# Attention and soft mixture of experts on one core: z loads at the batch turn, another order of v's low parts, x's shifts in a row

## The chip, the core and the metric

The kernel runs on one core of a Trainium2 chip. Its engines each work through a program of their own, in order: TensorE (PE in the profile, with its weight loads as PEld), VectorE (DVE), ScalarE (ACT), GpSimd (POOL) and SyncE (SP), which here issues the DMA transfers. They wait for one another by semaphores. The metric is the time of one execution in microseconds (us), the median over several runs.

## What is computed

Two stages, one behind the other. The first is an attention without softmax for 8 batches of 2496 tokens with 256 features: the scores are the products of z (64 features) with itself, cut at zero and squared, then multiplied with v and gated by u. The second is a soft mixture of experts over all 19968 rows of the first: 32 slots (8 experts with 4 each), with one softmax over the tokens to fill the slots, and another over the slots to give each token its output.

```python
def _attn_ref(u, v, z):
    scores = (1.0 / S) * np.matmul(z, z.transpose(0, 2, 1))
    attn = np.maximum(scores, 0.0) ** 2
    return u * np.matmul(attn, v)
...
def _moe_ref(x, phi, w1, w2):
    logits = x @ phi
    d = np.exp(logits - logits.max(0, keepdims=True))
    d /= d.sum(0, keepdims=True) + 1e-09
    slot_input = (d.T @ x).reshape(E, S_per_e, D)
    ...
    c = np.exp(logits - logits.max(1, keepdims=True))
    c /= c.sum(1, keepdims=True) + 1e-09
    return c @ slot_out
```

The numbers are single precision at the border. Inside, z, v and the squared scores are each kept as two 16-bit parts, a high one and a low one (what the high one has lost).

## The kernel before, in words

**Half steps.** A batch is worked in 5 chunks of up to 512 tokens as queries, and each chunk meets 5 blocks of 512 keys, each in two halves: 50 half steps per batch, numbered through the whole kernel, so that batch b begins at half step 50 b. A half step multiplies v (high and low part) with the squared scores (`ph` high, `pl` low) and adds the result up in PSUM (`acc`). PE's rows are `acc<-ph,v` and `acc<-pl,v`.

**Scores ahead.** While half step h is summed up, half step h+3 is prepared (`prepare`). PE makes the scores (`sc<-z,z`) in the middle of the sums of h. ACT cuts them at zero (`r<-sc`), squares them (`r<-r`) and casts the high part (`ph<-r`; in some half steps DVE casts). DVE subtracts the low part (`pl<-r,ph`). The tile `sc` exists once: the scores of the next half step are not written before ACT has read those of the last.

**Fetched half steps.** The scores are symmetric. DVE turns many `r` tiles around (`y<-r`), they are stored in DRAM (`turned<-y`) and later fetched as the mirrored half step (`r<-turned`), which then needs no scores. Quarter steps are lent and borrowed in the same way (`yd`, `lent`, `rd`).

**The second stage between the half steps.** When 1024 rows of x are there (`xg`, the gated sum, written by DVE at the end of a chunk), a group of the second stage starts. It has a list `todo`; one item is taken out per half step, as long as the half step is not among the first two of its chunk. Most items only put a function on one of two lists: `middle` is run in `prepare` right behind the next cut at zero, before its square, so on ACT; `behind` is run at the end of `prepare`, so behind the subtraction and the turning on DVE. The items are: `logits` (PE: x times phi, row `lg<-xg`, with the sums of the group before, `lg<-xt`, ahead of or behind them), `ex` (the first exp), four `blocks` and `e` (DVE turns x and the exponentials, `y<-xg`), four `shifts` (each four DMAs of 72 KB, `xt<-y`, by which x reaches the rows that the next sums need), `c0` the *combine* (three DVE operations on the tile `L`: a transposition, a maximum, a subtraction), `c1` the second exp (`L<-L` on ACT), `c2` sum and division, `c3` a last transposition. There are 18 groups with this list, each some 20 half steps behind the last.

**Loads of the next batch.** While batch b−1 runs, z and v of batch b are loaded (`zr<-in_zz`, `vr<-in_v`, 256 KB each, 12 places). A table gives the start (issue, two half steps ahead of it), and the half steps of what follows: for z the largest value (`sq<-zr`, DVE), then the split into parts; for v the squares, the high part on ACT (`v<-vr,v_by`) and the low part on DVE (`v<-vr,v_by,v`). In the code `base` is 50 (b−1).

**What sets the order.** Every engine's program is the order in which the code writes it, kept as it stands by a helper in line 78, so nearly all rows of the profile name that line. In a half step the code first does the transfers (`transfers(h)`, all on SP's queue, in order), then takes one item of a group's list, then adds the table's work that lands on this half step to `behind`, then writes the sums with the preparation of h+3 between:

```python
transfers(h)
if work and (x.at > 1 or last <= 20):
    work.pop(0)()
weights(last)
behind.extend(landing.pop(h, ()))
...
turn = sums_halves(h, acc, 0, None)
prepare(ahead.pop(0))
sums_halves(h, acc, 1, turn)
```

The lines that the change touches are 794 (the list of a group) and 903 to 906 (high and low parts of v, start of z).

Of the kernel before, what the change touches and what calls it, by code (L numbers as in the profile page):

```python
# [81 lines left out]
def attn_soft_moe_kernel(ctx, tc, uT, v, zz, zh, phi, ww, outT):  # L82
# [83 lines left out]
    def add_bounds(b, ps, js):  # L166
        pe.matmul(
            ps[:, 0, js], nc.const_aps.tensor(1.0, [P, P], F32), tops[b % 2][:, js], start=True, stop=True
        )

    def factors(b, ps, js):


        n2, by = (t[b % 2][:, js] for t in (norm2, z_by))
        dve.tensor_scalar(bits(n2), bits(ps[:, 0, js]), EVEN, None, op0=ALU.bitwise_and)
        dve.tensor_scalar(
            bits(by), bits(n2), EVEN, 1, op0=ALU.bitwise_xor, op1=ALU.logical_shift_right
        )
        dve.tensor_scalar_mul(by, by, 2.0**77)
# [25 lines left out]
    def largest(b):  # L205


        root, w = v_by[b % 2], few[b % 2]
        n2 = norm2[b % 2].unsqueeze(2).to_broadcast([P, NP, 2])
        dve.tensor_scalar(  # L210
            bits(root), bits(energy[b % 2]), 1, ROOT, op0=ALU.logical_shift_right, op1=ALU.bitwise_and
        )
        r2 = root.rearrange("p (j i) -> p j i", i=2)
        dve.tensor_tensor_reduce(
            r2, r2, n2, 1.0, 2.0**-120, op0=ALU.mult, op1=ALU.max, accum_out=w[:, 0:1]
        )

    def scale_v(b, ps):


        w = few[b % 2]
        ps = ps[:, :, 2 * PAD :]
        for h, rows in enumerate(HALF):
            pe.matmul(
                ps[:, h], w[rows, 0:1].to_broadcast([64, P]), ident[rows, rows],
                start=True, stop=True,
            )
        dve.tensor_reduce(w[:, 1:2], ps, axis=AX.XY, op=ALU.max)
        dve.tensor_scalar(
            bits(w[:, 2:3]), bits(w[:, 1:2]), EXPONENT, EXPONENT, op0=ALU.bitwise_and, op1=ALU.bitwise_xor  # L230
        )
        n2 = norm2[b % 2].unsqueeze(2).to_broadcast([P, NP, 2])
        dve.tensor_scalar(
            v_by[b % 2].rearrange("p (j i) -> p j i", i=2), n2, w[:, 2:3], 2.0**-51, op0=ALU.mult, op1=ALU.mult
        )
        dve.tensor_scalar(
            out_by[b % 2], norm2[b % 2], w[:, 1:2], 2.0**40 / S**2, op0=ALU.mult, op1=ALU.mult
        )
# [363 lines left out]
    def finish_chunk(b, ch, acc):  # L602
        j, _, n, t0 = ch
        ut = ut_.pop(t0)
        s = 0
        while s < n:
            q, o = divmod(t0 + s, 1024)
            w = min(n - s, 1024 - o)
            if q not in xg_:
                xg_[q] = wk.tile([P, 2, 1024], F32, tag="xg", name=f"xg_{q}")  # L610
            for c in (slice(0, 1), slice(1, 2)) if t0 + n == N else (slice(0, 2),):
                dve.scalar_tensor_tensor(
                    xg_[q][:, c, o : o + w], acc[:, c, s : s + w], out_by[b % 2][:, j : j + 1],
                    ut[:, c, s : s + w], op0=ALU.mult, op1=ALU.mult,
                )
            if o + w == 1024:
                work.extend(groups(q))
            s += w
# [17 lines left out]
    def shift(src, a):  # L636


        for b in range(4):
            sp.dma_start(xt[32 * b : 32 * b + 32, a], src[32 * a : 32 * a + 32, b])  # L640

    def groups(q):
# [48 lines left out]
        def turn_block(j, c):  # L691
            dve.transpose(
                y()[:, :, j * D : (j + 1) * D].rearrange("p b (t c f) -> p c t b f", t=4, c=2)[:, c],
                x[:, c, 512 * j : 512 * (j + 1)].rearrange("p (t b k) -> p t b k", t=4, b=4),
            )
# [50 lines left out]
        def turn_x_whole(i):  # L746
            j, t0 = i // 2, i % 2 * 2
            ps = ms_ps.tile([P, 2, 512], F32, tag="ms", name=f"xt_{q}_{i}")
            for k in range(2):
                turn_x(ps[:, k], x, 4 * j + t0 + k)  # L750
            for k in range(2):
                copy_x(act.copy, ps[:, k, 0:D], xt[:, t0 + k, j * D : (j + 1) * D])
# [34 lines left out]
        blocks = [lambda j=j, c=c: behind.append(lambda: turn_block(j, c)) for j in range(2) for c in range(2)]  # L787
        shifts = [lambda a=a: shift(y(), a) for a in range(4)]
        e, c0, c2, c3 = (lambda f=f: behind.append(f) for f in (turn_e, combine, combine_sum, combine_turn))
        ex, c1 = (lambda f=f: middle.append(f) for f in (exps, combine_exp))  # L790
        rest = lambda: None
        if q < NQG - 2:

            todo = [logits, ex, *blocks, e, *shifts[0:2], c0, *shifts[2:4], c1, c2]
            todo.append(lambda: (c3(), late.append(slot_sums)))
        else:


            todo = [rest, rest, logits, ex, lambda: behind.append(adding.pop(0)), lambda: behind.append(add_counts)]
            todo += [c0, c1, c2, c3, turn_e_whole, *[lambda i=i: turn_x_whole(i) for i in range(4)]]  # L800
            todo.append(lambda: late.append(last_slot_sums))
# [95 lines left out]
    splits, later = {}, {}  # L897
    for b in range(1, B):
        base, order = (b - 1) * 2 * NP * NQ, BLOCKS[b == B - 1]
        z_at = [28, 29, 30, 31, 39]  # L900
        v_from = [6, 7, 8, 9, 24, 25, 26, 31, 32, 33]
        v_sq = [17, 18, 19, 20, 28, 29, 30, 32, 33, 33]
        v_high = [43, 41, 41, 42, 42, 43, 44, 44, 45, 45]
        v_low = [47, 42, 43, 44, 45, 46, 48, 49, 50, 51]
        for i, (j, at) in enumerate(zip(order, z_at)):
            splits.setdefault(base + 9 + 2 * i, []).append((load_z, b, j, [base + 12 + 2 * i, base + at]))
        for i, (start, *steps) in enumerate(zip(v_from, v_sq, v_high, v_low)):
            splits.setdefault(base + start, []).append((load_v, b, i, [base + at for at in steps]))
        later[base + 23] = lambda b=b: add_bounds(b, next_acc(), slice(0, NP))
        later[base + 24] = lambda b=b: factors(b, accs[-1], slice(0, NP))  # L910
        later[base + 36] = lambda b=b: largest(b)
        later[base + 39] = lambda b=b: scale_v(b, ms_ps.tile([P, 2, 512], F32, tag="ms", name=f"mx_{b}"))
# [3 lines left out]
    def next_acc():  # L916

        accs.append(acc_ps.tile([P, 2, QC], F32, tag="acc", name=f"acc_{len(accs)}"))
        return accs[-1]
# [217 lines left out]
    for t in range(4):  # L1137
        pe.matmul(
            ep_[t * NS : (t + 1) * NS, 0:D], ET[:, t * NS : (t + 1) * NS], xt_last[t],
            start=True, stop=True,  # L1140
# [222 lines left out]
```

## Time and profile before

| | |
|---|---|
| median of 3 runs | 1285.04 us (1284.22 to 1287.97) |
| the profiled execution, its own time | 1285.79 us |
| its span | 1284.0 us |
| instructions on PE, DVE, ACT | 10987, 1582, 1211 |
| DMA | 299.41 MB, mean 233 GB/s |
| largest row: `acc<-ph,v` on PE, 5036 matmuls | 927.4 us |
| `acc<-pl,v` on PE, 2518 matmuls | 599.0 us |
| `pl<-r,ph` on DVE, 412 subtractions | 468.0 us |

The time of a row is its busy time. Matmuls overlap in the pipeline, so the rows of one engine may add up to more than the span. In a row of the timeline the columns are the start, the duration, the engine and the line, the operation with what it writes and reads, the shape and the count; a bracket at the end tells how long the engine had been idle before, and what it waited for. Rows of equal operations that follow each other are drawn together (x4). A wait "A <- B" in the list of waits says that the engine of A was idle until B was done.

### The profile page before, as it was taken

The page shows a single profiled execution, that of the slowest core. Times are in us where ns is not written, and L with a number is a line of the kernel's source. Part 1 is how long each engine was busy: PE and PEld are TensorE (multiplying, and loading weights), DVE is VectorE, ACT ScalarE, POOL GpSimd, SP SyncE. Part 2 cuts the span into 40 slices and gives each one's busy share as a digit, 9 for nine tenths or more (in the row PEclk, how much of TensorE's full clock was granted, in tenths as well). Part 3 has the DMA queues.
Part 4 walks back from the last instruction along what each step waited for, and adds up shares of the span by engine and source line. Part 5 has one row for each costly group of instructions (what it writes and reads, how often), then busy time and mean ns, then how long its engine had stood idle before and what let it go on. Part 6 is the DMA issues. An engine that isn't in the chain of part 4 may idle for free.

```text
span 1284.0 us, 27704 instructions
## 1 busy us (share of the span) xinstructions
PE 1250.8 (97%) x10987; PEld 597.8 (47%) x10987; DVE 1095.7 (85%) x1582; ACT 934.1 (73%) x1211; POOL 5.2 (0%) x23
## 2 busy tenths in 40 slices
PE   9999999999999999999999999999999999999984
PEld 3444444444444444444444444444444444445752
DVE  7888998889988899789998799898998899886663
ACT  7877786778866888677867778577876778564543
POOL 1000000000000000000000000000000000000000
PEclk9999999999999999999999999999999999999985
DMA  5768658774888758785787747877477758889869
GB/s 180 256 185 267 199 150 267 245 244 137 239 276 247 246 136 240 249 242 172 197 275 219 268 138 221 267 238 248 134 250 254 259 158 225 251 277 320 313 257 382
DMA packets 136546, 299.41 MB, mean 233 GB/s; under 512 B 17888, under 2 KB 38880, under 8 KB 124384
## 3 DMA queue, kind: packets, MB, share of 16 engines
q1 hardware_dynamic: 136416, 297.64, 73.1%
q8 instruction: 86, 1.41, 0.5%
q14 instruction: 44, 0.36, 0.1%
HBM read 162.56 MB, written 113.77 MB: 215 GB/s over the span
## 4 chain that ended last, share of the span: by engine, by line
PE 73%; DMA 9%; DVE 7%; ACT 5%; SPq 3%; issue 2%; ACTq 0%; DVEq 0%; POOLq 0%
PE acc L78 59%; PE sc L78 9%; SPq L78 3%; DMA r<-turned 3%; DVE pl L78 2%; PE lg L78 2%; DMA vr<-in_v 2%; PE pf L78 2%; DVE y L78 2%; ACT r L78 2%; DMA xt<-y 1%; DMA w_own<-in_w 1%; ACT ot L78 1%; ACT ph L78 1%; DMA turned<-y 1%
## 5 line engine op out<-in xcount | busy, mean ns | idle before, releaser
L78 PE MATMUL acc<-ph,v 64*128 64x512 f16 (+5 forms) x5036 | 927.4, 368 | 1.5 <-DVE v L78 1.2
L78 PEld LDWEIGHTS <-v 64*128 64x128 f16 (+1 forms) x7554 | 461.8, 95 | 531.6 <-issue 37.2
L78 PE MATMUL acc<-pl,v 64*128 64x512 f16 (+5 forms) x2518 | 599.0, 368 | 1.8 <-DVE pl L78 1.5
L78 DVE TENSOR_TENSOR pl<-r,ph 128x1024 f16<-128x1024 f32 (+1 forms) x412 | 468.0, 1141 | 110.6 <-ACT ph L78 88.2
L78 ACT CAST ph<-r 128x1024 f16<-128x1024 f32 (+1 forms) x286 | 289.5, 1016 | 147.5 <-DMA r<-turned 112.1
L78 ACT ACTIVATE r<-sc 128x1024 f32<-128x1024 f32 (+1 forms) x230 | 217.7, 947 | 107.0 <-PE sc L78 100.6
L78 ACT ACTIVATE r<-r 128x1024 f32<-128x1024 f32 (+1 forms) x242 | 238.5, 986 | 6.8
L78 DVE STREAM_TRANSPOSE y<-r 128x1024 f32<-128x1024 f32 x160 | 198.0, 1237 | 0.0
L78 PE MATMUL sc<-z,z 64*128 64x512 f16 x912 | 123.4, 376 | 1.5 <-ACT r L78 1.4
L78 PEld LDWEIGHTS <-z 64*128 64x128 f16 x1380 | 68.0, 94 | 75.8 <-issue 2.3
L78 DVE CAST ph<-r 128x1024 f16<-128x1024 f32 (+1 forms) x123 | 73.0, 594 | 14.5 <-ACT r L78 14.3
L78 ACT ACTIVATE v<-vr,v_by 128x512 f16<-128x512 f32 (+1 forms) x81 | 53.8, 707 | 10.2 <-DVE v_by L78 10.2
L78 DVE SCALAR_TENSOR_TENSOR xg<-acc,out_by,ut 128x1024 f32<-128x1024 f32 (+7 forms) x57 | 51.7, 929 | 8.4 <-PE acc L78 8.4
L78 DVE SCALAR_TENSOR_TENSOR v<-vr,v_by,v 128x512 f16<-128x512 f32 (+1 forms) x81 | 58.1, 718 | 0.0
L78 ACT ACTIVATE vq<-vr 128x512 bf16<-128x512 f32 x75 | 46.8, 623 | 15.5 <-DMA vr<-in_v 15.1
L78 PE MATMUL sc<-z 64*128 64x512 f16 (+1 forms) x468 | 50.6, 321 | 0.0
L78 DVE STREAM_TRANSPOSE y<-xg 128x512 f32<-128x512 f32 x72 | 49.4, 686 | 0.0
L78 DVE COPY ot<-pf 128x1024 f32<-128x1024 f32 (+1 forms) x20 | 24.0, 1198 | 20.5 <-PE pf L78 20.5
L78 ACT COPY ot<-pf 128x1024 f32<-128x1024 f32 (+1 forms) x20 | 19.8, 991 | 24.2 <-PE pf L78 24.2
L78 DVE TENSOR_TENSOR pl<-rd,ph 128x512 f16<-128x512 f32 x36 | 23.7, 660 | 6.4 <-ACT ph L78 6.4
L78 DVE SCALAR_TENSOR_TENSOR z<-zr,z_by,z 128x512 f16<-128x512 f32 x35 | 25.8, 737 | 0.0
L78 DVE STREAM_TRANSPOSE yd<-r 128x512 f32<-128x512 f32 x36 | 25.3, 704 | 0.0
(188 smaller groups left out, 541.8 us busy)
## 6 DMA issues: line engine op xcount, KB each, us to landing
turned<-y SPq DMA_DIRECT2D x320, 256.0 KB, 5.2
r<-turned SPq DMA_DIRECT2D x76, 1024.0 KB, 7.2
xt<-y SPq DMA_DIRECT2D x288, 72.0 KB, 4.2
vr<-in_v SPq DMA_DIRECT2D x80, 256.0 KB, 4.6
outT<-ot SPq DMA_DIRECT2D x18, 1024.0 KB, 6.7
ut<-in_uT SPq DMA_DIRECT2D x31, 512.0 KB, 6.6
lent<-yd SPq DMA_DIRECT2D x144, 64.0 KB, 2.6
rd<-lent SPq DMA_DIRECT2D x36, 256.0 KB, 5.0
```

The costliest lines, as they stand in the source:

```text
L78: return lambda *a, **k: self.tc.keep_in_program_order(f(*a, **k))
```

## The change

```diff
-            todo = [logits, ex, *blocks, e, *shifts[0:2], c0, *shifts[2:4], c1, c2]
+            todo = [logits, ex, *blocks, e, *shifts, c0, c1, c2]
...
-        v_high = [43, 41, 41, 42, 42, 43, 44, 44, 45, 45]
-        v_low = [47, 42, 43, 44, 45, 46, 48, 49, 50, 51]
+        v_high = [41, 43, 41, 42, 42, 43, 44, 44, 45, 45]
+        v_low = [42, 49, 43, 44, 45, 46, 46, 48, 52, 47]
         for i, (j, at) in enumerate(zip(order, z_at)):
-            splits.setdefault(base + 9 + 2 * i, []).append((load_z, b, j, [base + 12 + 2 * i, base + at]))
+            start = base + i - 1 if base else 9 + 2 * i
+            splits.setdefault(start, []).append((load_z, b, j, [base + 12 + 2 * i, base + at]))
```

In a group's list, shifts 2 and 3 come one half step earlier, and the combine comes two half steps later, directly ahead of the second exp, which keeps its place. Of v, part 0 is split earlier (low part at step 42 instead of 47 of the batch before), part 1 later (49 instead of 42), and parts 6 to 9 at 46, 48, 52 and 47 instead of 48, 49, 50 and 51. Of z, for batches 2 to 7, the five loads are issued at half steps base−3 to base+1 instead of base+7 to base+15; what is done with them stays where it was.

On DVE, in batch 2 around half step 106, group 3 (its `L` has the number 3819; `pl` and `y` with 43.. and 44.. are the half steps 107, 108 and 109). Before:

```order
L78 STREAM_TRANSPOSE L_3819<-L_3819 128x256
L78 TENSOR_REDUCE rm_3729<-L_3819 128x8
L78 TENSOR_TENSOR L_3819<-L_3819,rm_3729 128x256
L78 TENSOR_TENSOR pl_4316<-r_4305,ph_4315 128x1024
L78 STREAM_TRANSPOSE y_4319<-r_4305 128x2x16x32
L78 TENSOR_TENSOR pl_4368<-r_4357,ph_4367 128x1024
L78 STREAM_TRANSPOSE y_4319<-r_4357 128x2x16x32
L78 TENSOR_TENSOR pl_4411<-rd_4176,ph_4410 128x8x64
```

The same place now:

```order
L78 TENSOR_TENSOR pl_4327<-r_4316,ph_4326 128x1024
L78 STREAM_TRANSPOSE y_4330<-r_4316 128x2x16x32
L78 TENSOR_TENSOR pl_4375<-r_4364,ph_4374 128x1024
L78 STREAM_TRANSPOSE y_4330<-r_4364 128x2x16x32
L78 STREAM_TRANSPOSE L_3819<-L_3819 128x256
L78 TENSOR_REDUCE rm_3729<-L_3819 128x8
L78 TENSOR_TENSOR L_3819<-L_3819,rm_3729 128x256
L78 TENSOR_TENSOR pl_4421<-rd_4200,ph_4420 128x8x64
```

The three operations on `L` have moved behind the subtractions and transpositions of two half steps. ACT's rows around the second exp stand as before; here they are in the kernel now, where `r_4364` is half step 108 and `r_4409` half step 109:

```order
L78 CAST ph_4374<-r_4364 128x1024
L78 ACTIVATE r_4409<-sc_4410 128x2x256
L78 ACTIVATE L_3819<-L_3819 128x256
L78 ACTIVATE r_4409<-r_4409 128x2x256
L78 CAST ph_4420<-rd_4200 128x8x64
L78 ACTIVATE r_4456<-sc_4457 128x1024
```

The exp reads what the combine's subtraction writes, as it did, and the rest of ACT's work for half steps 109 and 110 stands behind it.

On DVE ahead of the turn at half step 150, from the low part of v5 to the gated rows `xg`. Before:

```order
L78 SCALAR_TENSOR_TENSOR v_5_4281<-vr_5_5068,v_by_90,v_5_4281 128x2x256
L78 CAST ph_5914<-r_5904 128x1024
...
L78 SCALAR_TENSOR_TENSOR v_0_4276<-vr_0_4286,v_by_90,v_0_4276 128x2x256
...
L78 SCALAR_TENSOR_TENSOR v_6_4282<-vr_6_5117,v_by_90,v_6_4282 128x2x256
...
L78 SCALAR_TENSOR_TENSOR v_7_4283<-vr_7_5332,v_by_90,v_7_4283 128x2x256
L78 SCALAR_TENSOR_TENSOR xg_5349<-acc_5716,out_by_91,ut_5753 128x2x128
```

And now:

```order
L78 SCALAR_TENSOR_TENSOR v_5_3965<-vr_5_5068,v_by_90,v_5_3965 128x2x256
L78 SCALAR_TENSOR_TENSOR v_6_3966<-vr_6_5118,v_by_90,v_6_3966 128x2x256
L78 CAST ph_5927<-r_5917 128x1024
...
L78 SCALAR_TENSOR_TENSOR v_9_3969<-vr_9_5381,v_by_90,v_9_3969 128x2x256
...
L78 SCALAR_TENSOR_TENSOR v_7_3967<-vr_7_5332,v_by_90,v_7_3967 128x2x256
...
L78 SCALAR_TENSOR_TENSOR v_1_3961<-vr_1_4344,v_by_90,v_1_3961 128x2x256
L78 SCALAR_TENSOR_TENSOR xg_5349<-acc_5716,out_by_91,ut_5753 128x2x128
```

Between the cast of half step 150 and `xg` stand three low parts in both, and two instead of one right ahead of that cast; v0 is not among them any more.

On SP's queue in the first steps of batch 2, where z of batch 3 is loaded. Before, z stands between the stores and fetches there:

```order
L78 DMA vr_2_4384<-in_v 128x512
L78 DMA zr_0_4428<-in_zz 128x512
L78 DMA vr_3_4430<-in_v 128x512
L78 DMA turned_0_4_4432<-y_4319 32x4x512 x4
L78 DMA lent_1_4476<-yd_4462 32x4x128 x4
L78 DMA zr_1_4523<-in_zz 128x512
L78 DMA rd_4571<-lent_1_4476 128x512
L78 DMA r_4614<-turned_0_1_4128 128x2048
L78 DMA zr_2_4616<-in_zz 128x512
```

Now the loads stand ahead of the batch's first stores:

```order
L78 DMA zr_0_3970<-in_zz 128x512
L78 DMA zr_1_4015<-in_zz 128x512
L78 DMA lent_0_4017<-yd_3999 32x4x128 x4
L78 DMA zr_2_4065<-in_zz 128x512
L78 DMA xt<-y_3874 32x576 x4
L78 DMA zr_3_4108<-in_zz 128x512
L78 DMA zr_4_4151<-in_zz 128x512
L78 DMA turned_0_1_4153<-y_4049 32x4x512 x4
```

The five loads have left the stretch with the fetches `r` and come behind the turn of the batch.

## The prediction

> **What bounds the kernel now.** I read the head of the page first, then the list of waits, then the timeline at the places that the change touches.
>
> ```profile
> span 1284.0 us, 27704 instructions
> ...
> PE 1250.8 (97%) x10987; PEld 597.8 (47%) x10987; DVE 1095.7 (85%) x1582; ACT 934.1 (73%) x1211; POOL 5.2 (0%) x23
> ...
> PEclk9999999999999999999999999999999999999985
> ...
> PE 73%; DMA 9%; DVE 7%; ACT 5%; SPq 3%; issue 2%; ACTq 0%; DVEq 0%; POOLq 0%
> ```
>
> TensorE (PE) is busy for 97% of the span at a granted clock of 0.9 or more in all slices but the last two, and the change takes no matmul away. So the kernel can only get faster where PE stands still, and gets slower wherever PE is made to stand. VectorE (DVE) at 85% and ScalarE (ACT) at 73% have room on average; what counts is whether they are late at one given matmul. The waits (total us, times, longest):
>
> ```profile
> ACT ph L78 <- DMA r<-turned: 112.1, 34, 8.5
> ACT r L78 <- PE sc L78: 102.1, 92, 3.8
> ...
> ACT L L78 <- DVE L L78: 7.6, 3, 3.0
> ...
> PE lg L78 <- DMA xt<-y: 2.0, 2, 1.3
> ...
> PE sc L78 <- ACT r L78: 1.4, 2, 1.1
> ...
> PE acc L78 <- DVE v L78: 1.2, 3, 0.7
> ...
> PE lg L78 <- DVE xg L78: 0.7, 1, 0.7
> ```
>
> The last four rows are PE's: 5.3 us in eight stalls (counted between starts, about 7 us, since the matmuls around a stall also stretch). They are at the four kinds of place that this change works on: the last shift of x (`xt<-y`), the scores' single tile (`sc<-z`), the low part of v0 at the batch turn, and the gated rows `xg`. That is all that the change can win in the middle of the kernel.
>
> The first two rows are the cover: ACT has often nothing to do until PE has made the next scores, or until a fetched `r` has landed. The third is the sign of danger: in 3 of its groups ACT's second exp (`L<-L`) already waits for the three combine operations of DVE.
>
> **The change part by part.** *Part 1, four shifts in a row, combine behind them.* The combine (a transpose, a reduce and a subtract on `L`) moves two half steps later; the exp that reads its result stays where it is. The instructions are the same, 19 times each:
>
> ```profile
> L78 ACT ACTIVATE L<-L x19: 398/407/417, 131.7 to 1192.7; 128x256 f32<-128x256 f32 x19
> ```
>
> Of these, 18 belong to groups with the changed list. Groups are some 20 half steps long and batches 50, so the exp falls on steps 6, 26, 46, 16 and 36 of a batch in turn; the eighteenth, behind the others, waits for nothing. I take step 6 first, group 3, where the exp stands at half step 106. First DVE, then ACT, then PE:
>
> ```profile
> 332.61 0.40 DVE L78 STREAM_TRANSPOSE L<-L 128x256 f32<-128x256 f32 x1
> 333.05 0.42 DVE L78 TENSOR_REDUCE rm<-L 128x8 f32<-128x256 f32 x1
> 333.50 0.42 DVE L78 TENSOR_TENSOR L<-L,rm 128x256 f32<-128x256 f32 x1
> 333.85 1.22 DVE L78 TENSOR_TENSOR pl<-r,ph 128x1024 f16<-128x1024 f32 x1
> 334.98 1.24 DVE L78 STREAM_TRANSPOSE y<-r 128x1024 f32<-128x1024 f32 x1
> ...
> 337.24 1.23 DVE L78 STREAM_TRANSPOSE y<-r 128x1024 f32<-128x1024 f32 x1
> ```
>
> ```profile
> 333.98 1.04 ACT L78 CAST ph<-r 128x1024 f16<-128x1024 f32 x1
> 334.93 0.59 ACT L78 ACTIVATE r<-sc 128x512 f32<-128x512 f32 x1
> 335.42 0.41 ACT L78 ACTIVATE L<-L 128x256 f32<-128x256 f32 x1
> 335.73 0.62 ACT L78 ACTIVATE r<-r 128x512 f32<-128x512 f32 x1
> 336.25 0.60 ACT L78 CAST ph<-rd 128x512 f16<-128x512 f32 x1
> 337.78 1.02 ACT L78 ACTIVATE r<-sc 128x1024 f32<-128x1024 f32 x1 [0.92 <-PE sc L78]
> ```
>
> ```profile
> 339.73 0.81 PE L78 MATMUL sc<-z,z 64*128 64x512 f16 x6
> ```
>
> Now the combine is done at 333.9 and the exp finds it ready at 335.42. Afterwards DVE starts `pl` of half step 107 at 332.61, in the combine's place. The `pl` of 108 must wait for ACT's cast, which ends at 335.02, so it runs to 336.2, its transpose to 337.4, and only then comes the combine, 1.24 us from 332.61 to 333.85 by the rows, now 337.4 to 338.65. The exp starts at 338.70, **3.3 us later**. Behind it on ACT, in program order, stand the square, the cast of the fetched half and the relu of the next scores. From the exp's start to that relu the rows need 0.31 + 0.52 + 0.52 = 1.35 us, so the relu begins at 340.05 instead of 337.78 and ends at 341.07. ACT's own wait of 0.92 us is used up and 2.3 us are left over. The score tile has one copy: PE's next scores, due at 339.73, must wait until this relu has read it. The old relu ended at 338.80, so 0.93 us of lateness were free; 1.4 us become a stall of PE. That such a wait stops PE at once shows in a place of before:
>
> ```profile
> 719.68 1.00 ACT L78 ACTIVATE r<-sc 128x1024 f32<-128x1024 f32 x1
> ...
> 720.74 0.61 PE L78 MATMUL sc<-z,z 64*128 64x512 f16 x4 [1.08 <-ACT r L78]
> ```
>
> The relu ended at 720.68 and the scores came 0.06 us later. Step 6 comes four times (groups 1, 3, 8, 13), with the same rhythm of rows: 4 × 1.4 = **+5.6 us**. Bounds: 4 if DVE gains 0.4 us each time, 6.4 if the matmuls after a stall stretch by 0.2 us.
>
> At steps 26 and 36 the DVE transposition behind which the combine now lands begins at, for example,
>
> ```profile
> 576.94 1.24 DVE L78 STREAM_TRANSPOSE y<-r 128x1024 f32<-128x1024 f32 x1
> ```
>
> ```profile
> 694.99 1.24 DVE L78 STREAM_TRANSPOSE y<-r 128x1024 f32<-128x1024 f32 x1
> ```
>
> and the exp, at 576.16 and 694.21 before, comes near 579.5 and 697.5. But the half steps that follow there use fetched `r` and need no scores, so the score tile is no limit; late are only the casts `ph` and the subtractions `pl` of the half step with the fetched half. Following the rows by the same rule, PE waits about 0.9 us at each of the three steps 26, and has its later stalls there shrunk by nearly as much, as PE itself then comes later: +1.2 together. Steps 36 (groups 0, 2, 7, 12): 0.3, 0.3, 1.1, 0.7, together +2.4. At step 16 the exp waits already, and ACT idles for its fetches there:
>
> ```profile
> 513.07 0.42 DVE L78 TENSOR_TENSOR L<-L,rm 128x256 f32<-128x256 f32 x1
> ...
> 513.53 0.42 ACT L78 ACTIVATE L<-L 128x256 f32<-128x256 f32 x1 [2.33 <-DVE L L78]
> ```
>
> I put it at +0.5 for all three. Bounds of these ten places: 0.5 to 8 us.
>
> *Part 2, low parts of v.* Ten subtractions per batch as before; only the order changes. Before, the turns at half steps 150 and 350 looked so (DVE, then PE):
>
> ```profile
> 460.19 0.75 DVE L78 SCALAR_TENSOR_TENSOR v<-vr,v_by,v 128x512 f16<-128x512 f32 x1
> ...
> 467.03 1.27 DVE L78 SCALAR_TENSOR_TENSOR xg<-acc,out_by,ut 128x256 f32<-128x256 f32 x2
> ```
>
> ```profile
> 467.36 1.25 PE L78 MATMUL lg<-xg,phi_sb 64*32 64x256 f32 x32
> ```
>
> ```profile
> 1057.31 0.36 PE L78 MATMUL acc<-ph,v 64*128 64x448 f16 x2 [0.69 <-DVE v L78]
> ...
> 1064.41 0.87 PE L78 MATMUL lg<-xg,phi_sb 64*32 64x256 f32 x22 [0.73 <-DVE xg L78]
> ```
>
> The low part of v0 ended at 460.94, just when PE wanted it; moved to step 42 it is early, and the stalls at the three turns with a group's exp (half steps 150, 250, 350) go: 0.32, 0.50 and 0.85 us between starts, −1.7. But step 46 now has two low parts, so DVE carries one more of them (0.65 us from its start to the next) into the turn, and there the combine too stands one exp later, which holds ACT, and with it DVE's inputs, by 0.75 to 0.95 us. I get `xg` 1.15, 1.5 and 0.7 us later than before, while PE comes earlier by the stalls that went. PE was 0.1 us behind `xg` at 467.36 and already waited at 1064.41, so this lands on PE: 1.5, 1.9, 1.55, less the stalls won = **+3.25 us net**. Bounds 1.5 to 5. At the other four turns no logits follow at once on `xg`, and I count nothing; that cover gone, they would cost up to 0.65 us each.
>
> *Part 3, z loads at the turn.* Thirty DMAs move 10 to 14 half steps earlier past SP's queue. Who waits for them is nobody:
>
> ```profile
> L78 SPq DMA_DIRECT2D zr<-in_zz x35: 377/433/2137, 39.7 to 968.0; - x35
> ```
>
> Behind this row the view lists no engine that sat idle for `zr`, before or after. The Trainium skill ("DMA: Bandwidth & Descriptors", Rules for kernel authors) advises to issue a DMA early and wait for it late, by which this part would pay for itself; the list of waits has no row for z, so the rule finds nothing to win here. What the part does give is room: 0.43 us of SP's queue per load is gone from the half steps where shifts and fetches stand. Together with the earlier fourth shift this removes the two stalls for it:
>
> ```profile
> 530.41 0.59 PE L78 MATMUL lg<-xt 64*32 64x256 f32 x2 [0.66 <-DMA xt<-y]
> ```
>
> ```profile
> 829.54 0.80 PE L78 MATMUL lg<-xt 64*32 64x256 f32 x10 [1.34 <-DMA xt<-y]
> ```
>
> Those are 0.66 + 1.34 = 2.0, with the stretch about 2.4: I take **−2.2 us**, bounds −2.4 and, if the shift is still late, 0. At the turn the loads join `lent` and the stores; their slots are long free, and I count 0, with up to 1 us if they hold up a store.
>
> **Sum:** 5.6 + 1.2 + 2.4 + 0.5 + 3.25 − 2.2 = +10.75 us. The profiled execution took 1285.79 us (span 1284.0 and 1.8 around it), so 1296.5 for the same execution; it lies 0.75 above the median 1285.04, so near **1296 us** as a median. Lowest terms together: 4 + 0.5 + 1.5 − 2.4 = +3.6, 1289. Highest: 6.4 + 8 + 5 + 0 = +19, 1304, but not all at once.
>
> **The rivals.**
>
> *A, the delay is covered* (ends faster). ACT waited 102 us in all for scores, and if DVE reached the combine early enough, the exp would be late by less than the free lateness and cost nothing. Then only the removals act: shifts −2.2, v0 −1.7, the two score stalls −1.6 (0.32 and 1.08 plus stretch, if ACT has more room there): −5.5, **1279.5 us**. The point from which it decides is in the rows: the relu may be 0.93 us late, and with ACT's 0.92 us of idle time the exp may slip by 1.85. I work out 3.3, because `pl` of 108 waits for a cast that ends at 335.02, whatever DVE does earlier. So DVE would have to be 1.45 us faster from there, which no row supports.
>
> *B, gains and losses cancel.* The step 6 stalls come (+5.6), while the fine terms at steps 26, 36 and at the turn are absorbed by PE's later arrival, and all removals of A come: 5.6 − 5.5, **1285 us**. For it speaks that my fine terms are each below 1.5 us and rest on long chains; against it, that DVE is loaded at 85% and catches up slowly.
>
> *C, the queue.* Sixteen small DMAs of a group now stand closer together:
>
> ```profile
> L78 SPq DMA_DIRECT2D xt<-y x288: 507/589/2504, 115.1 to 1175.8; - x144
> ```
>
> Four of one shift take 4 × 0.59 = 2.4 us of SP, and a fetch of `r` behind them starts that much later. ACT's waits for fetched `r` (112 us, 34 times) show that some fetches land just in time; with 1 to 2.4 us at three or four of them the sum rises by about 5: **1301 us**. The Trainium skill ("Perfetto Trace Analysis", What "DMA-bound" means) names an issuing engine whose track is solid with DMA issues as a bound of its own; the fetches that this would delay are followed by idle time of ACT rather than of PE in the waits above, so I give it little.
>
> *D, nothing is late or won.* The shifts came in time but for two places and z never mattered; if the exp's wait fell on idle time and the queue kept the two stalls, only v0's 1.7 us would be left: 1283.5. I count it with B.
>
> **How the numbers follow.** A difference of 0.3%, 3.9 us, is about what a measurement of this kernel can tell from no change. Forecast (+4 to +17 us): 0.70. A: 0.10. B with D: 0.15. C: 0.05. The range takes in the lower bound of the sum, most of B, and C: 1284 to 1302; A, D and the extreme ends, some 0.17, stay outside. Faster: A, and little of B: 0.12. Same: the rest of B, and the forecast's low end, where only step 6 costs something: 0.16. Slower: 0.72.
>
> **What would show it.** Right: the row "ACT L <- DVE L" grows from 3 times to about 15 with some 2 to 3 us each; a new PE wait `sc <- ACT r` of about 1 us at half steps 58, 108, 208 and 308; the waits of PE for `xt` and for v0 gone; `lg <- DVE xg` up to three times with 1 to 2 us, two half steps behind 150, 250 and 350. Wrong: the exp waits, yet `sc` starts on time (A); PE's waits at the turns missing (B); or long waits of ACT for `r<-turned` that reach PE (C). What would break the whole reckoning is a DVE that reaches the combine much earlier than the casts let it, so that its start at step 6 is below 336.

## The result and the profile after

| | before | changed |
|---|---|---|
| median of 6 runs | 1286.1 us (1284.22 to 1289.76) | 1303.84 us (1302.48 to 1307.89) |
| ratio, 95% interval | | 1.0145 (1.0128 to 1.0161) |
| profiled execution, its own time | 1285.79 us | 1307.89 us |
| its span | 1284.0 us | 1306.1 us |

The changed kernel is slower by 17.7 us in the medians; 1296 us was forecast, with a range up to 1302. Its profiled execution is the longest of its six, 4 us above their median, so the parts below, which are read from it, add up to 22 us and not to 17.7.

The head of the page of the changed kernel, with the chain that ended last:

```profile
span 1306.1 us, 27670 instructions
...
PE 1255.0 (96%) x10987; PEld 601.3 (46%) x10987; DVE 1095.9 (84%) x1582; ACT 933.8 (71%) x1211; POOL 5.1 (0%) x23
...
PE 60%; DVE 14%; ACT 10%; DMA 9%; issue 4%; SPq 2%; DVEq 0%; ACTq 0%
```

The work is the same; PE's share of the chain fell from 73% to 60%, and DVE's and ACT's rose from 12% to 24% together. So the chain now leads through these two more often. The list of waits names the places where PE waits for them (total us, times, longest):

```profile
ACT L L78 <- DVE L L78: 57.5, 19, 5.7
...
PE lg L78 <- DVE few L78: 6.1, 4, 1.5
...
PE sc L78 <- ACT r L78: 4.9, 4, 1.2
PE acc L78 <- DVE v L78: 4.6, 2, 4.5
...
PE lg L78 <- DVE xg L78: 2.7, 2, 1.6
...
PE acc L78 <- ACT ph L78: 2.3, 1, 2.3
```

Now every one of the 19 second exps waits for the combine, where 3 did before. The wait for `xt` is gone. The second row and the last are new, and no step of the prediction had them.

PE runs the same 10987 matmuls in nearly the same order in both kernels. So the start of its n-th matmul, after less before, tells at each place how much has been lost up to there. Worked out from the two traces, it rises and falls only at these places:

| place | forecast | from the traces |
|---|---|---|
| steps 6 to 8, four times | +5.6 | 1.41 + 1.40 + 1.39 + 1.40 = +5.6 |
| steps 36 to 41, four times | +2.4 | 1.93 + 2.05 + 3.20 + 2.43 = +9.6 |
| steps 26 to 32, with the old score stalls that go | +1.2 | 0.21 + 0.49 + 0.48 − 1.25 = −0.1 |
| step 16 | +0.5 | 0 |
| turns at half steps 150 and 250 | +2.55 | 1.27 + 1.29 = +2.6 |
| turn at half step 350, to the last batch | +0.7 | +4.8 |
| last shift of x, two places | −2.2 | −1.23 − 1.89 = −3.1 |
| behind half step 387, last groups | 0 | +2.6 |
| sum | +10.75 | +22.0 |

**Steps 6 to 8.** Timeline of the changed kernel at the place that the prediction worked out (group 3), ACT, DVE and PE:

```profile
343.99 0.42 ACT L78 ACTIVATE L<-L 128x256 f32<-128x256 f32 x1 [3.19 <-DVE L L78]
344.31 0.61 ACT L78 ACTIVATE r<-r 128x512 f32<-128x512 f32 x1
344.83 0.60 ACT L78 CAST ph<-rd 128x512 f16<-128x512 f32 x1
345.33 1.01 ACT L78 ACTIVATE r<-sc 128x1024 f32<-128x1024 f32 x1
```

```profile
342.64 0.40 DVE L78 STREAM_TRANSPOSE L<-L 128x256 f32<-128x256 f32 x1
343.07 0.42 DVE L78 TENSOR_REDUCE rm<-L 128x8 f32<-128x256 f32 x1
343.53 0.42 DVE L78 TENSOR_TENSOR L<-L,rm 128x256 f32<-128x256 f32 x1
345.46 0.69 DVE L78 TENSOR_TENSOR pl<-rd,ph 128x512 f16<-128x512 f32 x1 [1.51 <-ACT ph L78]
```

```profile
346.40 0.82 PE L78 MATMUL sc<-z,z 64*128 64x512 f16 x6 [1.23 <-ACT r L78]
```

The exp waits 3.19 us for the subtraction on DVE, the relu behind it ends at 346.34, and PE's scores start 0.06 us later. Note the bracket at DVE's 345.46: DVE first made ACT wait, and then stands idle for 1.51 us itself, since the cast that it needs stood behind the waiting exp. This loss of DVE harms nobody here, but it does at the next place.

**Steps 36 to 41.** The same in group 7, DVE, then PE, of the changed kernel:

```profile
588.39 0.69 DVE L78 TENSOR_TENSOR pl<-rd,ph 128x512 f16<-128x512 f32 x1 [1.51 <-ACT ph L78]
...
598.74 0.28 DVE L78 TENSOR_REDUCE few<-mx 128x1 f32<-128x128 f32 x1
```

```profile
599.08 1.10 PE L78 MATMUL lg<-xg,phi_sb 64*32 64x256 f32 x32 [1.54 <-DVE few L78]
```

and of the kernel before, DVE and PE:

```profile
588.36 0.28 DVE L78 TENSOR_REDUCE few<-mx 128x1 f32<-128x128 f32 x1
```

```profile
588.86 1.10 PE L78 MATMUL lg<-xg,phi_sb 64*32 64x256 f32 x32
```

The tile `mx` (from which DVE takes the maximum for v's scale) and the logits' tile `lg` come from one pool of PSUM tiles, `ms`. The logits cannot be written before DVE has read `mx`. The pool holds one such tile at a time. Before the change DVE was done at 588.64, and PE came at 588.86 without waiting. At the four places 0.2 to 0.4 us lay between. The list of waits of the kernel before has one hint of it, in the row of the logits' weight loads:

```profile
PEld lg L78 <- DVE few L78: 1.5, 4, 0.4
```

That row is no loss: PEld idles as long, 0.4 us, ahead of the logits of most other groups, where nothing is waited for. But it says that `few` was the last thing to be done there. After the change DVE's 1.5 us of idle time go to PE nearly whole: between 588.39 and 598.74 DVE has no other idle time in which to catch up. In two of the four batches (half steps 189 and 289) PE waits besides for the late `ph` of the half step itself, 1.13 and 0.35 us.

**The last turn.** DVE and PE of the changed kernel, behind half step 350:

```profile
1077.80 0.71 DVE L78 SCALAR_TENSOR_TENSOR v<-vr,v_by,v 128x512 f16<-128x512 f32 x1
1078.42 1.27 DVE L78 SCALAR_TENSOR_TENSOR xg<-acc,out_by,ut 128x768 f32<-128x768 f32 x2
```

```profile
1078.56 0.56 PE L78 MATMUL acc<-ph,v 64*128 64x448 f16 x2 [4.45 <-DVE v L78]
```

The row at 1077.80 is the low part of v1, now at step 49. In the last batch the first chunk meets its key blocks in another order than in the others, and v1 is needed in its second half step, 51, instead of 59. PE stands for 4.45 us.

**The last groups.** Here PE waits for `ph` of a fetched half step. ACT and SP of the changed kernel, then SP of the kernel before:

```profile
1202.67 1.89 ACT L78 CAST ph<-r 128x512 f16<-128x512 f32 x3 [8.88 <-DMA r<-turned]
```

```profile
1190.44 3.25 SPq L78 DMA_DIRECT2D xt<-y  x4
...
1194.86 2.84 SPq L78 DMA_DIRECT2D xt<-y  x4
1197.80 1.01 SPq L78 DMA_DIRECT2D r<-turned  x2
```

```profile
1170.16 2.41 SPq L78 DMA_DIRECT2D xt<-y  x4
1172.67 0.53 SPq L78 DMA_DIRECT2D r<-turned  x1
1173.24 3.13 SPq L78 DMA_DIRECT2D xt<-y  x4
```

A shift that stood behind the fetch now stands ahead of it. Before, the fetch was issued 8.7 us ahead of the matmul that needs it (at 1181.41); now it is 5.5 us (1203.34), and PE waits for the last 2.33 of them. This is what rival C had described, at one place.

### The profile page after: what moved, and what is told of

Read it like the earlier page. It is cut to its first block, busy times and chain, and to the rows that moved or that the text cites. A ratio compares the mean times of both kernels' runs of the same rounds, so it can differ in the third digit from the quotient of the medians.

```text
span 1306.1 us, 27670 instructions
## 1 busy us (share of the span) xinstructions
PE 1255.0 (96%) x10987; PEld 601.3 (46%) x10987; DVE 1095.9 (84%) x1582; ACT 933.8 (71%) x1211; POOL 5.1 (0%) x23
## 3 DMA queue, kind: packets, MB, share of 16 engines
q8 instruction: 86, 1.41, 0.4%
## 4 chain that ended last, share of the span: by engine, by line
PE 60%; DVE 14%; ACT 10%; DMA 9%; issue 4%; SPq 2%; DVEq 0%; ACTq 0%
PE acc L78 47%; PE sc L78 7%; DVE pl L78 5%; ACT r L78 4%; DVE y L78 3%; ACT ph L78 3%; DMA r<-turned 3%; PE lg L78 2%; SPq L78 2%; DMA vr<-in_v 2%; PE pf L78 2%; DMA turned<-y 1%; ACT ot L78 1%; DMA rd<-lent 1%; DVE ph L78 1%
## 5 line engine op out<-in xcount | busy, mean ns | idle before, releaser
L78 ACT ACTIVATE L<-L 128x256 f32<-128x256 f32 x19 | 7.9, 416 | 57.5 <-DVE L L78 57.5
L78 PE MATMUL lg<-xg,phi_sb 64*32 64x256 f32 x608 | 22.0, 382 | 8.8 <-DVE few L78 6.1
```

The lines of the kernel that those rows point to most:

```text
L78: return lambda *a, **k: self.tc.keep_in_program_order(f(*a, **k))
```

## The experiments

Theory 1: the loss comes from the combine standing in the half step directly ahead of the exp, which holds ACT and by it DVE, and at the last turn from v1. Theory 2, in several forms: it comes from z's loads, from the shifts in a row, or from v. Each experiment is compared with the kernel before, run on the same chip.

**The three parts alone.** The list alone, on the kernel before:

```diff
-            todo = [logits, ex, *blocks, e, *shifts[0:2], c0, *shifts[2:4], c1, c2]
+            todo = [logits, ex, *blocks, e, *shifts, c0, c1, c2]
```

> Only the group's list is changed (four shifts in a row, combine directly ahead of the second exp); v's order and z's loads as before. Theory 1 (the late combine holds ACT and through it DVE): nearly all of the loss comes with it: four score stalls at steps 6 to 8 of a batch (1.4 us each), four waits of the logits for the maximum of v at steps 36 to 41 (about 2.4 us each with what goes ahead), some 2 us in the last groups, less the late shifts: +13 to +17 us, ratio 1.010 to 1.013. Theory 2 (the loss at steps 36 to 41 and in the last groups comes from z or v): only the score stalls, +4 to +6 us, ratio 1.003 to 1.005.

Measured: 1301.21 us against 1286.09, ratio 1.0121 (1.0096 to 1.0146). Its waits:

```profile
ACT L L78 <- DVE L L78: 57.7, 19, 5.7
...
PE lg L78 <- DVE few L78: 6.1, 4, 1.5
...
PE sc L78 <- ACT r L78: 5.4, 5, 1.2
```

The exp's 19 waits, the four waits for `few` and the four score stalls (and a fifth, of 0.4 us) come with the list alone, with the same lengths as in the changed kernel. Theory 2 falls for these places.

The order of v alone:

```diff
-        v_high = [43, 41, 41, 42, 42, 43, 44, 44, 45, 45]
-        v_low = [47, 42, 43, 44, 45, 46, 48, 49, 50, 51]
+        v_high = [41, 43, 41, 42, 42, 43, 44, 44, 45, 45]
+        v_low = [42, 49, 43, 44, 45, 46, 46, 48, 52, 47]
```

> Only the order of v's high and low parts is changed. Theory 1: PE waits for the low part of v1 once, at the turn to the last batch, where the second half step needs it: about +4.5 us there, less the short stalls for v0 at half steps 150 and 250, in all +3 to +5 us, ratio 1.0025 to 1.004, and no wait of the logits for the maximum of v. Theory 2 (the stall at the last turn needs the late combine too): within 1 us of before.

Measured: 1290.87 us, ratio 1.0039 (1.0021 to 1.0056), +4.8 us. The stall for v1 is there with 4.36 us, without any late combine; the logits wait for `xg` at half steps 150 and 250 with 0.60 and 0.29 us, and for `few` nowhere.

z's loads alone:

```diff
-            splits.setdefault(base + 9 + 2 * i, []).append((load_z, b, j, [base + 12 + 2 * i, base + at]))
+            start = base + i - 1 if base else 9 + 2 * i
+            splits.setdefault(start, []).append((load_z, b, j, [base + 12 + 2 * i, base + at]))
```

> Only z's loads are moved to the batch turn. Theory 1: nobody waits for z, and SP's queue gets free where the last shift was late: 0 to -2.5 us, ratio 0.998 to 1.000. Theory 2 (loads at the turn hold up fetches or stores): +3 us or more, with longer waits of ACT for r at the start of batches.

Measured: 1286.68 us, ratio 0.9996 (0.9978 to 1.0014): no difference, at the upper end of what was expected. Its profile shows gains and losses side by side. The two stalls for `xt` that the kernel before had are gone (a new one of 0.83 us stands in the last groups), and so is its score stall of 1.08 us; but two other score stalls are longer. ACT and PE of this run:

```profile
418.13 1.04 ACT L78 CAST ph<-r 128x1024 f16<-128x1024 f32 x1 [2.48 <-DMA r<-turned]
```

```profile
423.93 0.82 PE L78 MATMUL sc<-z,z 64*128 64x512 f16 x6 [1.85 <-ACT r L78]
```

A fetched `r` was used at 418.13 instead of 417.11, and the next scores waited 1.85 us instead of 0.32. A second such stall, 2.09 us, stands at 1017.64, where the kernel before had none. The fetches moved in the queue as well; which of its neighbours held them up was not tried. Nor is it shown that z's loads did all of this: the run with v's order alone, whose list and z are those of before, has no wait for `xt` either, and a stall of 1.03 us at the second place.

The three parts alone give 15.1 + 4.8 + 0.6 = 20.5 us, together they gave 17.7. The intervals of the single runs, 2 to 3 us to either side, are too wide to tell whether the parts cover each other.

**The place of the combine.** In the changed kernel, the combine ahead of all four shifts, then (the second run) behind the third:

```diff
-            todo = [logits, ex, *blocks, e, *shifts, c0, c1, c2]
+            todo = [logits, ex, *blocks, e, c0, *shifts, c1, c2]
```

> The changed kernel, but with the combine ahead of the four shifts (two half steps earlier than before the change) instead of behind them. Theory 1: the exp never waits, so the score stalls and the waits at steps 36 to 41 go; left are the stall for v1 at the last turn and the gain of the shifts: -1 to +4 us against before, ratio 0.999 to 1.003. Theory 2 (it is the shifts in a row or z, not the place of the combine): still +10 us or more, ratio above 1.008.

Measured: 1298.33 us, ratio 1.0089 (1.0064 to 1.0115), +12.2 us. That is a number that theory 2 allowed (+10 us or more), but the waits are not those that it would leave:

```profile
PE acc L78 <- DVE pl L78: 7.7, 13, 1.0
...
PE acc L78 <- DVE v L78: 4.5, 2, 4.3
...
PE sc L78 <- ACT r L78: 3.9, 4, 1.8
...
ACT L L78 <- DVE L L78: 3.0, 1, 3.0
```

The exp waits only once, the waits for `few` are gone and the score stalls of steps 6 to 8 too. But new ones came: thirteen waits of PE for `pl`, up to 1 us, since the 1.24 us of the combine now stand on DVE ahead of a subtraction that PE needs soon; and four score stalls at other places; the longest, of 1.8 us, stands where the kernel before had one of 1.08, with ACT still at squares of v. So the place ahead of the shifts has a price of its own.

```diff
-            todo = [logits, ex, *blocks, e, *shifts, c0, c1, c2]
+            todo = [logits, ex, *blocks, e, *shifts[0:3], c0, *shifts[3:4], c1, c2]
```

> The changed kernel, but with the combine one half step earlier: behind the third shift, with the fourth between it and the second exp. Theory 1 (the combine must not stand in the half step directly ahead of the exp): the exp is late by less than the 1.85 us that are free, the score stalls and the waits for the maximum of v go nearly all, left is the stall for v1 at the last turn less the shifts: +2 to +6 us against before, ratio 1.0015 to 1.005. Rival (shifts in a row or z are to blame, or any other place of the combine costs as much, as in the run with the combine ahead of the shifts): +10 us or more, ratio above 1.008.

Measured: 1287.43 us, ratio 1.0014 (1.0003 to 1.0026), +1.4 us, a little less than theory 1 had. One half step between combine and exp takes away 16.3 of the 17.7 us. The rows at the same place (group 3), DVE, ACT and PE, and its waits:

```profile
334.91 0.42 DVE L78 TENSOR_TENSOR L<-L,rm 128x256 f32<-128x256 f32 x1
```

```profile
335.37 0.42 ACT L78 ACTIVATE L<-L 128x256 f32<-128x256 f32 x1
...
337.48 1.02 ACT L78 ACTIVATE r<-sc 128x1024 f32<-128x1024 f32 x1 [0.67 <-PE sc L78]
```

```profile
339.44 0.81 PE L78 MATMUL sc<-z,z 64*128 64x512 f16 x6
```

```profile
ACT L L78 <- DVE L L78: 11.1, 3, 4.0
...
PE acc L78 <- DVE v L78: 4.1, 2, 3.9
...
PE lg L78 <- DVE xg L78: 1.5, 2, 1.0
PE sc L78 <- ACT r L78: 1.5, 2, 0.8
```

The combine ends at 335.33 and the exp starts 0.04 us later, after 0.14 us of idle time. The three waits that are left in the list stand where the kernel before had its three, and are longer. ACT has 0.67 us to spare again before the next scores, and PE writes those without a wait. The shifts in a row and the loads of z are the same as in the changed kernel but for the fourth shift, one half step later; so they are not to blame for these stalls. What is left is v's order.

**One kind of group at a time.** In the changed kernel, the old list in four groups: those with the exp on step 36 or 37, then those with step 6.

```diff
-            todo = [logits, ex, *blocks, e, *shifts, c0, c1, c2]
+            todo = [logits, ex, *blocks, e, *shifts[0:2], c0, *shifts[2:4], c1, c2]
+            if q not in (0, 2, 7, 12):
+                todo = [logits, ex, *blocks, e, *shifts, c0, c1, c2]
```

> The changed kernel, with the old list in groups 0, 2, 7 and 12 alone, whose second exp falls on step 36 or 37 of a batch. Theory 1: the late combine makes DVE late by some 1.5 us, DVE reads the maximum of v (row few<-mx) late from the PSUM tile that the next logits need, and PE waits for it: with the old list there the four waits lg <- DVE few and what goes ahead of them vanish, about -9 us against the changed kernel, so about +8 to +9 us against before, ratio 1.006 to 1.0075. Rival: the fault is z's or v's or the shifts' elsewhere in the batch and stays: +15 us or more, ratio above 1.011.

Measured: 1298.07 us, ratio 1.0091 (1.0076 to 1.0107), −5.8 us against the changed kernel, where theory 1 had about −9 and the rival next to nothing. The waits for `few` are gone from its list, the four score stalls stay (`PE sc <- ACT r`, 4.9 us, 4 times). By the starts of PE's matmuls its profile loses nothing at steps 36 to 41, where the changed kernel lost 9.6; in the last groups it loses nothing either, and the stall at the last turn is longer (+5.4 us instead of 4.8). In all this profile is 11.4 us shorter than that of the changed kernel; the medians show half of it, since this one is of the fastest of five executions, 1.5 us below their median, and that one of the slowest, 4 us above.

```diff
-            todo = [logits, ex, *blocks, e, *shifts, c0, c1, c2]
+            todo = [logits, ex, *blocks, e, *shifts[0:2], c0, *shifts[2:4], c1, c2]
+            if q not in (1, 3, 8, 13):
+                todo = [logits, ex, *blocks, e, *shifts, c0, c1, c2]
```

> The changed kernel, with the old list in groups 1, 3, 8 and 13 alone, whose second exp falls on step 6 of a batch. Theory 1: the four score stalls of 1.24 us vanish and nothing else changes: -5.6 us against the changed kernel, about +12 us against before, ratio 1.009 to 1.010. Rival: ACT's delay only moves to another wait there and the stall stays: +17 us, ratio 1.013.

Measured: 1303.35 us, ratio 1.0129 (1.0110 to 1.0148): by the medians hardly better than the changed kernel, as the rival had it. The profile (span 1298.7, 7.4 us shorter than that of the changed kernel) shows the stalls themselves gone:

```profile
PE lg L78 <- DVE few L78: 6.0, 4, 1.5
PE acc L78 <- DVE v L78: 5.9, 1, 5.9
```

There is no row `PE sc <- ACT r` left in it, and by the starts of PE's matmuls nothing is lost at steps 6 to 8. What the median shows against it is partly the stall at the last turn, longer by 1.4 us; for the rest this run can't tell, since executions of this kernel lie between 1299.38 and 1304.9.

**v1 in the last batch.** In the changed kernel:

```diff
+        if b == B - 1:
+            v_high[0:2], v_low[0:2] = [43, 41], [47, 42]
```

> The changed kernel, but with v0 and v1 of the last batch in the old half steps (low parts at 47 and 42). Theory 1: the stall of 4.45 us for v1 at the turn to the last batch, where v1 is needed in the second half step, goes and leaves one of about 1 to 1.6 us for v0: -3 to -4 us against the changed kernel, about +14 us against before, ratio 1.0105 to 1.0115. Rival: DVE is so late there that the stall only moves to xg: +17 us, ratio 1.013.

Measured: 1301.5 us, ratio 1.0121 (1.0103 to 1.0139), −2.3 us: by the number between theory 1 and the rival, and the interval shuts out neither. What decides is the profile. The wait for v at the last turn is 1.85 us instead of 4.45, with 0.72 us for `xg` behind it; by PE's starts this turn costs +1.2 us instead of +4.8.

**Who reads mx late.** In the changed kernel, the largest value and the scale of v one half step earlier:

```diff
-        later[base + 36] = lambda b=b: largest(b)
-        later[base + 39] = lambda b=b: scale_v(b, ...)
+        later[base + 35] = lambda b=b: largest(b)
+        later[base + 38] = lambda b=b: scale_v(b, ...)
```

> The changed kernel, but the maximum of v (the steps that read the energies and make few from the PSUM tile mx) one half step earlier, at 35 and 38 of a batch instead of 36 and 39. Theory 1: what PE waits for at steps 40 to 41 is only that DVE reads mx so late from the tile that the logits need; one half step (2.8 us) earlier it is read in time although DVE stays late: the four waits of 1.4 to 1.5 us vanish, -6 us against the changed kernel, about +11 us against before, ratio 1.008 to 1.010, the score stalls stay. Rival (DVE's lateness itself reaches PE by another operand there): the stalls only change their name, +16 us or more, ratio above 1.012.

Measured: 1300.11 us, ratio 1.0099 (1.0080 to 1.0118), +14 us against before, −3.7 against the changed kernel. Its waits:

```profile
PE sc L78 <- ACT r L78: 5.7, 5, 1.2
...
PE mx L78 <- DVE few L78: 4.1, 7, 1.2
```

The logits wait for `few` no longer, but PE now waits for the other value on DVE, `few` on the way into `mx`, seven times with up to 1.2 us. By PE's starts steps 36 to 41 cost 3.4 us here instead of 9.6. So it was the reading of `mx` that held the logits. The new waits are 0.43, 0.43, 1.15 and 1.16 us in the four batches with the exp at step 36, and about 0.3 us in the other three: the earlier place has a small price of its own, and a late DVE adds to it.

**A version that beats both.** The list with one half step between, z at the turn, v as before the change; and the same with v0 and v1 exchanged (`v_high` 41, 43 and `v_low` 42, 47 at their head):

> The list of the run with one half step between combine and exp, z's loads at the turn, but v's order as before the change. Theory 1 (what was left in that run is v's order): the stall of 4 us for v1 at the last turn and the waits for xg at the turns (0.5 and 1.0 us) go, the short stalls for v0 (0.3 to 0.9 us) come back, the two waits for the last shift stay away: 0 to -3 us against before, ratio 0.9977 to 1.0000. Rival (z at the turn costs something there too): +1 us or more, ratio above 1.001.

Measured: 1281.93 us, ratio 0.9965 (0.9951 to 0.9978), −4.2 us, somewhat more than the 0 to −3 that were expected. Its waits:

```profile
ACT L L78 <- DVE L L78: 13.4, 7, 4.0
...
PE acc L78 <- DVE v L78: 1.8, 3, 1.3
...
PE acc L78 <- DVE pl L78: 1.1, 2, 0.7
...
PE lg L78 <- DVE xg L78: 0.7, 1, 0.7
```

There are no waits for `xt`, for `sc` or for `few`.

> As the run before, but v0 and v1 exchanged in the order of before (low part of v0 at step 42, of v1 at 47), the others as before the change. Theory 1: as that run, and the short stalls for v0 at the turns go too, since v1 is needed one half step after v0 at the soonest: -2 to -4 us against before, ratio 0.997 to 0.9985. Rival (v1 is then as late at the last turn as v0 was, or DVE is late with xg whatever the order): no better than the run before.

Measured: 1283.76 us, ratio 0.9978 (0.9963 to 0.9992), no better than the run before, as the rival had it, though the ratio lies in the range of theory 1 too. The waits for v are gone from its list, and at the last turn one of 1.6 us for `xg` has come in their place.

## Why the prediction was right and wrong

- *Direction, and step 6: right.* The rows gave 1.4 us four times, the trace has 1.4 four times; the exp's wait was 3.19 us where 3.3 had been worked out. Rival A fell there: nothing covers a relu that is late by more than 0.93 us. B has these stalls too; it fell because the terms at steps 36 and at the last turn, which it took to be absorbed, cost 9.6 and 4.8 us.
- *Steps 36 and 37: the step that failed.* The prediction said "the half steps that follow there use fetched `r` and need no scores, so the score tile is no limit; late are only the casts `ph` and the subtractions `pl`", and priced that at +2.4 us for four places. It cost 9.6 us in the profiled execution, and 8.1 to 10.1 in the four profiles that have the late combine and the old place of `mx` there. DVE, idle for ACT's cast, comes 1.5 us late to all that stands behind, and one of those operations frees the PSUM tile of the logits. It had 0.2 us to spare, which a look at PE's next logits behind each late operation would have shown: `few` ended at 588.64, `lg` began at 588.86, and the list of waits named `few` at the weight loads. The run with the old list at steps 36 and the one with the maximum earlier carry this.
- *Part 2, the last turn: failed too.* The prediction put the three turns at +3.25 us together and saw only `xg`. For the turns at 150 and 250 that was right (2.55 against 2.6), but it took v1's new step 49 to be early enough for every batch, as it is for those that need v1 at step 59. In the last batch it is needed at 51: +4.8 us instead of 0.7, and +4.4 us of stall in the run with v's order alone.
- *The last groups: left out.* The prediction counted nothing for group 17; in the profiled execution PE lost 2.6 us there (row `PE acc <- ACT ph`, 2.3 us). In the runs with one half step between combine and exp the loss is not there; in the others with the late combine in this group it lies between nothing and 2.2 us. The cause is known as far as the late fetch; what makes it late stays open. The run with the combine first has the same two shifts ahead of the fetch and no wait, so their order alone is not enough; the late exp was not tried alone.
- *Steps 26 and the shifts: sized a little too high.* −0.1 instead of +1.2, and −3.1 instead of −2.2. That the earlier shift and the room in the queue removed the two waits for `xt` is not shown: they are missing with v's order alone as well.
- *Part 3: right in result.* The prediction counted 0 for z itself; z alone measured 0.9996 (0.9978 to 1.0014). The Trainium skill's advice to issue a DMA early ("DMA: Bandwidth & Descriptors", Rules for kernel authors) found nothing to win here, as the trace had no wait for z. With z alone, two waits for `xt` went and two score stalls behind late fetches grew; how much of either is the loads' doing stays open.
- *Rival C: right at one place.* In the changed kernel a late fetch reaches PE in the last groups, with 2.3 us, and nowhere else; the rest of the loss has other causes. The issuing queue as a bound of its own (the Trainium skill, "Perfetto Trace Analysis", What "DMA-bound" means) fits that stretch: from 1189.62 to this fetch at 1197.80 one DMA issue on SP follows the other with 0.1 us or less between them.
- *The sum.* Of the 11 us missing in the profiled execution, 7.2 are the steps 36, 4.1 the last turn, 2.6 the last groups; −1.3, −0.5 and −0.9 are the terms that were too high. The 4 us between this execution and the median of the six runs were not taken apart.

## What to carry to other kernels

When an operation is moved to stand just ahead of the one on another engine that needs it, the wait has to be followed through both engines: the second engine waits, then the first waits for the second, and what the first does next is late. For every operation that becomes late, look at who needs its result or the tile that it frees, and at what time: a row without a wait may have 0.2 us to spare or much more, and only the two timelines tell. A table of due times has to be held against every order in which the parts are used, the last pass's above all.

## What was not expected of the hardware

Nothing of the engines themselves. The stalls at steps 6 and 36 reproduce very closely from run to run: the four score stalls were 1.23 or 1.24 us long in all five profiles that have them, and the four waits for `few` 1.42 to 1.55 us in the four that have them. The executions of one kernel differ by up to 11 us (the kernel before, 1282.11 to 1293.55 in 23 executions); where that arises was not looked into.
